# Backward pass of two attention blocks on one core: dwo rows in a shared ring of four, an earlier load of the second block's x^T and g^T, and small moves at both ends

## The chip, the cores and the metric

The kernel runs on one core of a Trainium2 chip. A core has a matrix engine (TensorE, PE in the profile; its weight loads are PEld), VectorE (DVE), ScalarE (ACT), GpSimd (POOL), and SyncE (SP), which here does nothing but issue transfers. Sixteen DMA engines move the data between HBM and the on-chip memory SBUF; matmuls write to PSUM, which has eight banks. The metric is the device time of one execution in microseconds, as the median of several runs.

## The reference

Two independent attention blocks, A and B, have the same shapes: batch 8, 96 queries, width 640, 32 heads of 128, 512 cached keys per head. All inputs are bf16.

```python
q = (x @ wq).reshape(B, Sq, H, Dh).transpose(0, 2, 1, 3)
scores = einsum("bhqd,bhkd->bhqk", q, k_cache) * Dh ** -0.5
p = softmax(scores)
o = einsum("bhqk,bhkd->bhqd", p, v_cache)
out = o.transpose(0, 2, 1, 3).reshape(B, Sq, H * Dh) @ wo
```

The outputs of both blocks are joined on the last axis. The kernel must return this output and, for a given gradient g of it, the gradients of all ten inputs: dx, dK, dV, dwq and dwo of A and of B. dK and dV are as large as the caches (33.5 MB each), so most traffic is the caches in and their gradients out.

## The kernel before

**Cells.** The unit of work is a cell: one head of one batch element, 256 per block and 512 in all. In a cell TensorE computes the scores S (L313), P^T and O^T (L360, L367), dV (L385), dP and the row sums dl (L409, L411), dQ^T and dS^T (L428, L435) and dK (L451). VectorE takes the row maximum, the reciprocal of the row sum, copies O^T and dS^T out of PSUM and forms dS. ACT does the exponential E and copies P^T, dV, dQ^T and dK out of PSUM. POOL scales E to P (L344) and forms the product of O^T and dO^T (L399).

**Ticks.** The order of the work is written by hand. Every piece is a function put on a list with a tick and a slot within the tick (`em.add`); the list is sorted and the functions run in that order. One cell starts per tick; its stages are spread over the following nine (`OFF`: scores at +3, P^T and dV at +4, O^T at +5, dP at +6, dK at +8, dQ^T at +9). Block 1 starts at tick 20 and block 2 at tick 276. The two heads of a pair alternate. The work of a whole head lies between the cells: transposes of wo and wq (`pB`, L214), Q^T and dO^T (`pC`, L231), their natural layouts (`pD`), and after the cells O and dQ in natural layout (`qA`), dwo (`qB`, L479), dwq (`qD`), and the sums over heads for the output and dx (`gU`, L526), in groups of four heads. Its ticks are offsets from the head's first tick, in the tables `HK`, `HK1`, `HK2` and `HKE`; `HKE` serves heads 30 and 31 of block 1. The framework then orders the instructions of each engine by priority, those of S, E and P before others, and makes an instruction that needs a new buffer wait until the last user of the old one has finished. Each engine carries out its instructions in order.

**Queues.** All transfers go through SP, in the order of the list: `Chain` (L62) ties each to the one before. A transfer that waits, or takes long to issue, holds all later ones. K^T and V^T are loaded by transposing transfers (L276), K and V as they are (L287), dV and dK are stored per pair of cells (L296). dV has four buffers, dK three.

**Buffers that matter here.** A ring of three buffers of [128, 640] bf16, named `ob`, holds the staged rows of g for block 2 (`setup_stage`, L137), the transposed wo of the first two heads, and the output rows of the last group of each block (`gU`, L537). The dwo rows have one buffer of that size, `dwo_sb` (L484): ACT fills it in two pieces (widths 128 and 512), SP stores it (L495) a tick or two later, and the next head's first piece must wait for that store to land. For most heads the first piece lies eight ticks after the last head's; for heads 29 and 30 of block 1 it is five (ticks 277 and 282), and head 29's row is stored at the start of tick 282.

**The handover.** Block 2 needs x^T (five transposing loads, `setup_xT`, ticks 262 to 266) and g^T. For g^T the six row tiles of g are loaded into `ob` at ticks 264 (three) and 269 (three) and transposed by TensorE four ticks later (`setup_T`, ticks 268 and 273). x^T and g^T have one buffer each, so they are loaded after the last use by block 1, in `pC` of head 31 (ticks 259 to 262).

**The start.** TensorE first transposes the row tiles of x against the identity (`tp_ps`, L158), then computes Q^T (`q_ps`, L249).

Of the kernel before, what the change touches and what calls it, by code (L numbers as in the profile page):

```python
# [7 lines left out]
ACT = mybir.ActivationFunctionType  # L8
ALU = mybir.AluOpType
# [35 lines left out]
HP = 2  # L45
# [4 lines left out]

HK1 = [dict(HK[0], pB=2, pC0=[-8, -6], pC1=[3, 3], pD1=3.5, pD0=6), dict(HK[1], pB=2, pC0=[-8, -6], pC1=[3, 3.6], pD1=4, pD0=7)]
HK2 = [dict(HK[0], pB=-5, pC0=[-6, -4], pC1=[-1, 0], pD1=1, pD0=2, qB=[28, 27]), dict(HK[1], pC0=[-2, 0], pC1=[1, 2])]
HKE = [dict(HK[0], qB=[23, 22]), dict(HK[1], qA0=25, qA1=27, qB=[29, 28], qD=[(30, 0, 2), (31, 2, 4), (32, 4, 5)])]
GT0, NG0, NX0 = 0, 15, 18
EV = dict(pB0="act", pB1="dve", pC00="act", pC01="act", pC10="act", pC11="dve", pD0="dve", pD1="dve", qA0="dve", qA1="dve", qB0="act", qB1="act", qD="dve", gU="act")
GSPREAD0 = 9
# [20 lines left out]
def build_block(tc, em, tick0, blk, x, kc, vc, wq, wo, g_all, out_all, dx, dk, dv, dwq, dwo, ident, ones, pools, HG=4, first=True, groups=None):  # L77
# [58 lines left out]

    def setup_stage(t):  # L137
        def f():
            S[("g_nat", t)] = wk.tile([128, D], BF16, name="ob", bufs=3)
            sp(nc.sync.dma_start(S[("g_nat", t)][:], g_flat[t * 128:(t + 1) * 128, :]))  # L140
        return f

# [33 lines left out]
    if first:  # L176
        for t in range(TT):
            late = t * 128 >= tsplits[0][1]
            em.add(tick0 - 15, SL_LOAD + (2 if late else 0), setup_nat(0, t, t + 1))
            em.add(tick0 - (7 if late else 9), SL_HEAD, setup_T(0, t))  # L180
            em.add(tick0 + GT0, SL_LOAD - 2, setup_nat(1, t, t + 1))
            em.add(tick0 + GT0, SL_HEAD + (2 if late else -1), setup_T(1, t))
    else:
        for c in range(DC):
            em.add(tick0 - 14 + c, SL_LOAD + 0.5, setup_xT(c))
        for t in range(TT):
            tt = tick0 - 8 + 5 * (t // 3)
            em.add(tt - 4, SL_LOAD + 0.5, setup_stage(t))
            em.add(tt, SL_HEAD - 1, setup_T(1, t))
        for t in range(TT):  # L190
            em.add(tick0 + NG0 + t, SL_LOAD + 0.5, setup_nat(1, t, t + 1))
            em.add(tick0 + NX0 + 2 * t, SL_LOAD + 0.6, setup_nat(0, t, t + 1))
# [21 lines left out]
    def pB(h):  # L214
        def f():
            st = HS[(blk, h)]
            woT_ps = bank([128, DC * 128], BF16, "woT_ps")
            for c in range(DC):
                nc.tensor.transpose(woT_ps[:, c * 128:(c + 1) * 128], st["wo_h"][:, c * 128:(c + 1) * 128], ident[:])
            woT_h = wk.tile([128, D], BF16, name="ob", bufs=3) if first and h < HP else hd.tile([128, D], BF16, name="woT_h", bufs=1)  # L220
# [118 lines left out]
    def c_s3b(h, b):  # L339
        def f():  # L340
            with tc.high_priority(PRIO_OFF):
                st = CS[(blk, h, b)]
                P_sb = wk.tile([Sq, Sk], BF16, name="P_sb", bufs=5)
                nc.gpsimd.tensor_scalar(P_sb[:], st["E_sb"][:], st["rinv"][:], 0.0, op0=ALU.mult, op1=ALU.add)  # L344
                st["P_sb"] = P_sb
        return f

# [70 lines left out]
    def c_s78(k8, k7):  # L418
        def f():
            x_ps = bank([128, 1024], BF16, "dq_dst_ps")  # L420
            dq_view = None
            if k8 is not None:
                st = CS[(k8[0], k8[1], k8[2])]
                hs = HS[(k8[0], k8[1])]
                tok = slice(k8[2] * Sq, (k8[2] + 1) * Sq)
                dQT_ps = x_ps[:, 0:2 * Sq].bitcast(F32)
                for c in range(KC):
                    nc.tensor.matmul(dQT_ps, st["K_sb"][:, c, :], st["dST_sb"][:, c * Sq:(c + 1) * Sq], start=(c == 0), stop=(c == KC - 1))  # L428
                dq_view = (dQT_ps, hs, tok)
            if k7 is not None:  # L430
                st7 = CS[(k7[0], k7[1], k7[2])]
                dS_sb = st7["dS_sb"]
                dST_ps = x_ps[:, 256:256 + KC * Sq]
                for c in range(KC):
                    nc.tensor.transpose(dST_ps[:, c * Sq:(c + 1) * Sq], dS_sb[:, c * 128:(c + 1) * 128], ident[0:Sq, 0:Sq])  # L435
                dST_sb = wk.tile([128, KC * Sq], BF16, name="dST_sb", bufs=3)
                nc.vector.tensor_copy(dST_sb[:], dST_ps)  # L437
                st7["dST_sb"] = dST_sb
            if dq_view is not None:
                dQT_ps, hs, tok = dq_view  # L440
                nc.scalar.activation(hs["dQT_h"][:, tok], dQT_ps, ACT.Identity, scale=scale)
        return f

    def c_s7(h, b):
# [34 lines left out]
    def qB(h, di):  # L479
        def f():  # L480
            st = HS[(blk, h)]
            Onat = st["Onat"]
            if "dwo_sb" not in st:
                st["dwo_sb"] = hd.tile([128, D], BF16, name="dwo_sb", bufs=1)  # L484
            dwo_sb = st["dwo_sb"]
            (c0, w) = dsplits[di]
            w_ps = bank([128, w], F32, "dwo_ps")
            for t in range(TT):
                nc.tensor.matmul(w_ps[:], Onat[:, t, :], S["g_nat"][:, t, c0:c0 + w], start=(t == 0), stop=(t == TT - 1))  # L489
            evac(EV["qB%d" % di], dwo_sb[:, c0:c0 + w], w_ps[:])  # L490
        return f
# [33 lines left out]
    def gU(g, which, t, di):  # L525
        def f():  # L526
            acc = S.get("out_acc" if which == 0 else "dx_acc")
            (c0, w) = dsplits[di]
            o_ps = bank([128, w], F32, "o_ps")
            for hh in range(groups[g]):  # L530
                h = GH0[g] + hh
                src = HS[(blk, h)]["OT_h"] if which == 0 else HS[(blk, h)]["dQT_h"]
                rhs = G[g]["wo_r"][:, hh, c0:c0 + w] if which == 0 else HS[(blk, h)]["wqT_h"][:, c0:c0 + w]
                nc.tensor.matmul(o_ps[:], src[:, t * 128:(t + 1) * 128], rhs, start=(hh == 0), stop=(hh == groups[g] - 1))  # L534
            if g == NG - 1:
                if di == 0:
                    G[(g, which, t)] = wk.tile([128, D], BF16, name="ob", bufs=3)  # L537
                dst = G[(g, which, t)][:, c0:c0 + w]
            else:
                dst = acc[:, t, c0:c0 + w]  # L540
            if g == 0:
                evac(EV["gU"], dst, o_ps[:])
            else:
                nc.vector.tensor_tensor(dst, o_ps[:], acc[:, t, c0:c0 + w], op=ALU.add)
        return f
# [80 lines left out]
def _kernel_impl(tc, A_x, A_k_cache, A_v_cache, A_wq, A_wo, B_x, B_k_cache, B_v_cache, B_wq, B_wo, grad_out,  # L626
# [13 lines left out]
    with ExitStack() as ctx:  # L640
        P = lambda **kw: ctx.enter_context(tc.tile_pool(**kw))
        cst = P(name="gconst", bufs=1)
        ident = cst.tile([128, 128], BF16, name="ident")
        make_identity(nc, ident[:])
        ones = cst.tile([128, 1], BF16, name="ones")
        nc.vector.memset(ones[:], 1.0)
        pools = dict(
            const=P(name="const", bufs=1),
            ps=P(name="ps", bufs=8, space=PSUM),
            kvp=P(name="kv", bufs=11),  # L650
            wk=P(name="wk", bufs=3),
            hd=P(name="hd", bufs=2),
            hst=P(name="hst", bufs=8),
            grp=P(name="grp", bufs=1),
        )
        pools["sp"] = Chain(tc)
        pools["S45"] = {}
        pools["S78"] = {}
        pools["HS"] = {}
        pools["CS"] = {}  # L660
        em = Emitter()
        t_next = 20
        for blk, args in enumerate(((A_x, A_k_cache, A_v_cache, A_wq, A_wo, grad_out, out_0, out_1, out_2, out_3, out_4, out_5),
                                    (B_x, B_k_cache, B_v_cache, B_wq, B_wo, grad_out, out_0, out_6, out_7, out_8, out_9, out_10))):
            H_ = args[1].shape[1]
            if blk == 0:
                grps = groupsA
# [72 lines left out]
```

## Time and profile before

| | |
|---|---|
| time, median of 5 runs | 1644.88 us (1640.71 to 1646.73) |
| the profiled execution | 1644.44 us, span 1642.7 us |
| mean granted TensorE clock | 0.996 |
| TensorE busy, idle in the span | 1611.6 us, 31.1 us |
| VectorE, ACT, POOL busy | 1337.4, 1350.8, 534.8 us |
| moved by DMA | 458.12 MB, mean 279 GB/s |
| store of a dwo row, issue to landing | 1.8 / 4.5 / 6.7 us (least, median, most) |
| transfers of the ring `ob`, issue to landing | 1.8 / 3.5 / 5.6 us |

The page gives one execution: busy time by engine, the chain of work that ended last, and groups of instructions with their mean duration and what ended the idle time before them. A row of the waits reads "engine, line waited for, releaser: total us, times, longest". A row of the timeline begins with the start and length in us; a bracket at its end is the idle time of that engine just before and what ended it. A row of the windows gives a stretch, its length, the busy time of PE, PEld, DVE, ACT and POOL with numbers of instructions, the granted TensorE clock (1 is full), the busy share of the DMA engines and GB/s.

### The profile page before, as it was taken

The numbers are of one execution on the slowest core, as the hardware profiler recorded it, in microseconds if no ns is written. First come the engines' busy times: TensorE is split into PE (matmuls) and PEld (weight loads), VectorE is DVE, ScalarE is ACT, GpSimd is POOL, SyncE is SP. The second block draws the span as 40 slices with busy tenths as digits, with TensorE's granted clock in tenths as the row PEclk, the third lists the DMA queues.
The fourth block names the chain that finished last, engine by engine and source line by source line (L and its number), as shares of the span: only waits on it lengthen the run. The fifth ranks groups of instructions, "written<-read, shape, count | busy, mean of one in ns | idle before, by whom it ended". The sixth has DMA issues, their size and how long they took to land.

```text
span 1642.7 us, 55592 instructions
## 1 busy us (share of the span) xinstructions
PE 1611.6 (98%) x20890; PEld 1261.4 (77%) x20890; DVE 1337.4 (81%) x3386; ACT 1350.8 (82%) x3514; POOL 534.8 (33%) x1030
## 2 busy tenths in 40 slices
PE   8999999999999999999989999999999999999998
PEld 5787877878777777777767777777787777877776
DVE  5786888888888888888768778888888888888896
ACT  6898988879788788888768889788798888889783
POOL 2332333333333333333223333333333333333331
PEclk9999999999999999999999999999999999999999
DMA  9999999999999999999999999999999999999994
GB/s 257 267 283 277 284 290 293 274 290 262 285 290 283 290 264 290 286 292 254 298 276 279 286 289 287 289 286 289 284 291 282 285 285 278 278 295 267 284 271 163
DMA packets 375566, 458.12 MB, mean 279 GB/s; under 512 B 40704, under 2 KB 367104, under 8 KB 367104
## 3 DMA queue, kind: packets, MB, share of 16 engines
q1 hardware_dynamic: 375296, 454.57, 102.5%
q8 instruction: 163, 2.67, 0.7%
q14 instruction: 107, 0.88, 0.1%
HBM read 160.10 MB, written 159.12 MB: 194 GB/s over the span
## 4 chain that ended last, share of the span: by engine, by line
PE 90%; ACT 4%; DMA 2%; DVE 1%; issue 1%; POOL 1%; SPq 0%; ACTq 0%; DVEq 0%
PE o_ps L534 12%; PE q_ps L249 12%; PE dV_ps L385 6%; PE dK_ps L451 6%; PE dwq_ps L509 6%; PE dwo_ps L489 6%; PE S_ps L313 6%; PE dP_ps L409 6%; PE optp_ps L360 6%; PE optp_ps L367 5%; PE dq_dst_ps L428 5%; PE dq_dst_ps L435 5%; PE n_ps L264 3%; PE nat_ps L475 3%; ACT E_sb L325 1%
## 5 line engine op out<-in xcount | busy, mean ns | idle before, releaser
L399 POOL TENSOR_TENSOR prod<-OT_h,dOT_h 128x96 bf16<-128x96 bf16 x512 | 187.1, 366 | 812.4 <-DVE rinv L335 452.8
L344 POOL TENSOR_SCALAR P_sb<-E_sb,rinv 96x512 bf16<-96x512 bf16 x512 | 352.4, 688 | 264.6 <-DVE rinv L335 264.2
L456 ACT ACTIVATE dK_sb<-dK_ps 128x512 bf16<-128x512 f32 x512 | 306.2, 598 | 141.9 <-PE dK_ps L451 126.4
L315 DVE TENSOR_REDUCE negm<-S_ps 96x1 f32<-96x512 f32 x512 | 347.7, 679 | 68.0 <-PE S_ps L313 67.6
L325 ACT ACTIVATE E_sb<-S_ps,negm 96x512 bf16<-96x512 f32 x512 | 352.1, 688 | 61.3 <-DVE negm L315 47.9
L413 DVE SCALAR_TENSOR_TENSOR dS_sb<-dP_ps,dl_ps,P_sb 96x512 bf16<-96x512 f32 x512 | 380.6, 743 | 1.1 <-PE optp_ps L367 0.8
L390 ACT ACTIVATE dV_sb<-dV_ps 128x512 bf16<-128x512 f32 x512 | 308.2, 602 | 4.6 <-PE dV_ps L385 2.6
L374 ACT ACTIVATE PT_sb<-optp_ps 128x384 bf16<-128x384 bf16 x512 | 256.2, 500 | 2.2 <-DVE OT_h L371 1.4
L437 DVE COPY dST_sb<-dq_dst_ps 128x384 bf16<-128x384 bf16 x512 | 177.8, 347 | 55.5 <-PE dq_dst_ps L435 53.9
L409 PE MATMUL dP_ps<-VT_p,dOT_h 128*96 128x512 bf16 x512 | 196.1, 383 | 4.9 <-ACT dwo_sb L169 4.9
L385 PE MATMUL dV_ps<-dOnat_h,P_sb 96*128 96x128 bf16 x2048 | 200.0, 219 | 0.0
L451 PE MATMUL dK_ps<-Qnat_h,dS_sb 96*128 96x128 bf16 x2048 | 199.0, 219 | 0.0
L313 PE MATMUL S_ps<-KT_p,QT_h 128*96 128x512 bf16 x512 | 194.2, 379 | 1.1 <-ACT dK_sb L456 0.4
L451 PEld LDWEIGHTS <-dS_sb 96*128 96x128 bf16 x2048 | 147.6, 97 | 48.4 <-issue 0.6
L367 PE MATMUL optp_ps<-ident,P_sb 96*128 96x96 bf16 x2048 | 172.6, 206 | 3.5 <-POOL P_sb L344 3.3
L428 PE MATMUL dq_dst_ps<-dST_sb,K_sb 128*128 128x96 bf16 x2048 | 172.0, 205 | 2.4 <-ACT dK_sb L456 2.4
L360 PE MATMUL optp_ps<-PT_sb,V_sb 128*128 128x96 bf16 x2048 | 169.6, 204 | 4.7 <-ACT PT_sb L374 2.6
L435 PE MATMUL dq_dst_ps<-ident,dS_sb 96*128 96x96 bf16 x2048 | 172.0, 205 | 0.0
L534 PE MATMUL o_ps<-wqT_h,dQT_h 128*128 128x512 bf16 (+1 forms) x768 | 149.3, 299 | 0.0
L534 PE MATMUL o_ps<-wo_r,OT_h 128*128 128x512 bf16 (+1 forms) x768 | 149.3, 299 | 0.0
L360 PEld LDWEIGHTS <-V_sb 128*128 128x128 bf16 x2048 | 107.7, 96 | 51.2 <-issue 3.9
L249 PE MATMUL q_ps<-xT,wq_p 128*128 128x256 bf16 (+1 forms) x640 | 135.4, 330 | 2.2 <-DMA wq_p<-in_A_wq_dram 1.4
(71 smaller groups left out, 3056.4 us busy)
## 6 DMA issues: line engine op xcount, KB each, us to landing
out_dram<-dV_sb SPq DMA_DIRECT2D x256, 256.0 KB, 4.4
out_dram<-dK_sb SPq DMA_DIRECT2D x256, 256.0 KB, 4.3
V_sb<-in_A_v_cache_dram SPq DMA_DIRECT2D x128, 256.0 KB, 4.4
K_sb<-in_A_k_cache_dram SPq DMA_DIRECT2D x128, 256.0 KB, 4.1
V_sb<-in_B_v_cache_dram SPq DMA_DIRECT2D x128, 256.0 KB, 4.1
K_sb<-in_B_k_cache_dram SPq DMA_DIRECT2D x128, 256.0 KB, 4.3
out_dram<-dwo_sb SPq DMA_DIRECT2D x64, 160.0 KB, 4.5
out_dram<-dwq_sb SPq DMA_DIRECT2D x32, 320.0 KB, 4.5
```

The source lines that it names most:

```text
L249: nc.tensor.matmul(q_ps[:], lhs(c), rhsT[:, c, t0:t0 + w], start=(c == 0), stop=(c == DC - 1))
L315: nc.vector.tensor_reduce(negm[:], S_ps[:], axis=AX.X, op=ALU.max, negate=True)
L325: nc.scalar.activation(E_sb[:].rearrange("q (a f) -> q a f", f=F4), st["S_ps"][:].rearrange("q (f a) -> q a f", f=F4), ACT.Exp, bias=st["n ...
L344: nc.gpsimd.tensor_scalar(P_sb[:], st["E_sb"][:], st["rinv"][:], 0.0, op0=ALU.mult, op1=ALU.add)
L360: nc.tensor.matmul(OT_ps, st["V_sb"][:, c, :], st["PT_sb"][:, c * Sq:(c + 1) * Sq], start=(c == 0), stop=(c == KC - 1))
L385: nc.tensor.matmul(dV_ps[:, c * 128:(c + 1) * 128], P_sb[:, c * 128:(c + 1) * 128], hs["dOnat_h"][:, b * 128:(b + 1) * 128], start=True, s ...
L390: nc.scalar.activation(dV_p[:, j], dV_ps[:], ACT.Identity, scale=1.0)
L409: nc.tensor.matmul(dP_ps[:], hs["dOT_h"][:, tok], st["VT"], start=True, stop=True)
L413: nc.vector.scalar_tensor_tensor(dS_sb[:].rearrange("q (a f) -> q a f", f=F4), dP_ps[:].rearrange("q (f a) -> q a f", f=F4), dl_ps[:, 0:1] ...
L451: nc.tensor.matmul(dK_ps[:, c * 128:(c + 1) * 128], dS_sb[:, c * 128:(c + 1) * 128], hs["Qnat_h"][:, b * 128:(b + 1) * 128], start=True, s ...
L456: nc.scalar.activation(dK_p[:, j], dK_ps[:], ACT.Identity, scale=1.0)
L534: nc.tensor.matmul(o_ps[:], src[:, t * 128:(t + 1) * 128], rhs, start=(hh == 0), stop=(hh == groups[g] - 1))
```

## The change

The ring `ob` has four buffers instead of three, and the dwo rows of all heads are taken from it; their own buffer is gone, so the memory is the same. Block 2's x^T is loaded at ticks 259, 260, 262, 263 and 265, its g rows at 261 and 266, and g is transposed at 265 and 270. To free x^T and g^T in time, heads 30 and 31 of block 1 do their transposes, Q^T and dO^T one to four ticks earlier, and head 31's wo is loaded three ticks earlier. At the start TensorE multiplies the identity by itself sixteen times into a PSUM bank that nobody reads. P of the first four cells (two heads, two batch elements) is scaled on VectorE instead of POOL. In the 16 cells of heads 30 and 31 of block 2, dQ^T is scaled and copied out of PSUM by VectorE instead of ACT.

```diff
-HKE = [dict(HK[0], qB=[23, 22]), dict(HK[1], qA0=25, qA1=27, qB=[29, 28], qD=[(30, 0, 2), (31, 2, 4), (32, 4, 5)])]
+HKE = [dict(HK[0], pB=-8, pC0=[-7, -6], pC1=[-6, -5], qB=[23, 22]),
+       dict(HK[1], pA=-10, pB=-4, pC0=[-4, -3], pC1=[-3, -2], pD1=2, pD0=5, qA0=25, qA1=27, qB=[29, 28], qD=[(30, 0, 2), (31, 2, 4), (32, 4, 5)])]
...
-            S[("g_nat", t)] = wk.tile([128, D], BF16, name="ob", bufs=3)
+            S[("g_nat", t)] = wk.tile([128, D], BF16, name="ob", bufs=4)
...
         for c in range(DC):
-            em.add(tick0 - 14 + c, SL_LOAD + 0.5, setup_xT(c))
+            em.add(tick0 - 17 + (3 * c) // 2, SL_LOAD + 0.5, setup_xT(c))
         for t in range(TT):
-            tt = tick0 - 8 + 5 * (t // 3)
+            tt = tick0 - 11 + 5 * (t // 3)
             em.add(tt - 4, SL_LOAD + 0.5, setup_stage(t))
             em.add(tt, SL_HEAD - 1, setup_T(1, t))
...
-                nc.gpsimd.tensor_scalar(P_sb[:], st["E_sb"][:], st["rinv"][:], 0.0, op0=ALU.mult, op1=ALU.add)
+                eng = nc.vector if first and h < HP and b * HP + h < 4 else nc.gpsimd
+                eng.tensor_scalar(P_sb[:], st["E_sb"][:], st["rinv"][:], 0.0, op0=ALU.mult, op1=ALU.add)
...
-                nc.scalar.activation(hs["dQT_h"][:, tok], dQT_ps, ACT.Identity, scale=scale)
+                evac("dve" if k8[0:2] in pools["light"] else "act", hs["dQT_h"][:, tok], dQT_ps, scale)
...
-                st["dwo_sb"] = hd.tile([128, D], BF16, name="dwo_sb", bufs=1)
+                st["dwo_sb"] = wk.tile([128, D], BF16, name="ob", bufs=4)
...
-                    G[(g, which, t)] = wk.tile([128, D], BF16, name="ob", bufs=3)
+                    G[(g, which, t)] = wk.tile([128, D], BF16, name="ob", bufs=4)
...
+        warm_ps = pools["ps"].tile([128, 128], F32, name="warm_ps", tag="bank")
+        for _ in range(16):
+            nc.tensor.matmul(warm_ps[:], ident[:], ident[:], start=True, stop=True)
         pools["sp"] = Chain(tc)
+        NH = A_k_cache.shape[1]
+        pools["light"] = {(1, h) for h in range(NH - HP, NH)}
```

More of the change, by code (lines that the diff above doesn't have):

```diff
@@ L219, in f @@
                 nc.tensor.transpose(woT_ps[:, c * 128:(c + 1) * 128], st["wo_h"][:, c * 128:(c + 1) * 128], ident[:])
-            woT_h = wk.tile([128, D], BF16, name="ob", bufs=3) if first and h < HP else hd.tile([128, D], BF16, name="woT_h", bufs=1)
+            woT_h = wk.tile([128, D], BF16, name="ob", bufs=4) if first and h < HP else hd.tile([128, D], BF16, name="woT_h", bufs=1)
             evac(EV["pB0"], woT_h[:], woT_ps[:])
```

## The prediction

> **What bounds the kernel now.** I read the page's sums first, then TensorE's waits, then the timeline where those waits lie, then SP's rows there, then the tail by windows.
>
> ```profile
> PE 1611.6 (98%) x20890; PEld 1261.4 (77%) x20890; DVE 1337.4 (81%) x3386; ACT 1350.8 (82%) x3514; POOL 534.8 (33%) x1030
> PE 90%; ACT 4%; DMA 2%; DVE 1%; issue 1%; POOL 1%; SPq 0%; ACTq 0%; DVEq 0%
> ...
> PE dP_ps L409 <- ACT dwo_sb L169: 4.9, 1, 4.9
> PE dq_dst_ps L428 <- ACT dK_sb L456: 2.4, 1, 2.4
> PE woT_ps L219 <- ACT dK_sb L456: 2.2, 1, 2.2
> PE tp_ps L158 <- DMA ob<-in_grad_out_dram: 1.2, 1, 1.2
> ```
>
> The first two lines are engine sums and the chain of waits: TensorE is the bound, so an edit gains only what it takes out of TensorE's idle time or out of slow-clock time. The other lines are single waits (total, times, longest). The edits aim at a few microseconds in three places.
>
> ```profile
> 782.15 2.19 SPq L140 DMA_DIRECT2D ob<-in_grad_out_dram  x3
> 786.78 1.28 PE L158 MATMUL tp_ps<-ident,ob 128*128 128x128 bf16 x15 [1.22 <-DMA ob<-in_grad_out_dram]
> 791.49 0.60 ACT L456 ACTIVATE dK_sb<-dK_ps 128x512 bf16<-128x512 f32 x1 [3.11 <-DMA out_dram<-dK_sb]
> 792.13 0.60 PE L219 MATMUL woT_ps<-ident,wo_r 128*128 128x128 bf16 x5 [2.15 <-ACT dK_sb L456]
> ...
> 821.12 1.15 SPq L495 DMA_DIRECT2D out_dram<-dwo_sb  x1
> 826.24 0.28 ACT L169 ACTIVATE dwo_sb<-dwo_ps 128x128 bf16<-128x128 f32 x1 [7.50 <-DMA out_dram<-dwo_sb]
> 826.57 0.58 PE L409 MATMUL dP_ps<-VT_p,dOT_h 128*96 128x512 bf16 x1 [4.88 <-ACT dwo_sb L169]
> ```
>
> This is the timeline where block 1 hands over to block 2 (start, length, engine; in brackets the idle time and its releaser). At 821.12 SP issues the store of one dwo row. ACT's next dwo evacuation needs the only dwo buffer, so it sits 7.50 us until that store lands, and TensorE runs dry for 4.88 us.
>
> ```profile
> 788.80:792.20 3.40, 1.25 (x25) 1.03 (x23) 1.27 (x4) 0.71 (x2) 0.36 (x1) 1.00 1.03 210
> 792.20:795.70 3.50, 3.50 (x17) 1.90 (x17) 1.90 (x4) 2.30 (x7) 0.69 (x1) 0.51 1.06 286
> 823.00:826.40 3.40, 0.00 (x0) 0.00 (x0) 0.00 (x0) 0.16 (x1) 0.00 (x0) 1.00 0.92 300
> 826.40:829.80 3.40, 3.23 (x19) 1.91 (x19) 0.99 (x3) 2.38 (x7) 1.05 (x2) 0.50 1.08 352
> ```
>
> In these windows (PE, PEld, DVE, ACT, POOL busy, granted clock, DMA share, GB/s) each of the two long gaps is followed by 3.4 us at clock 0.50. Work of 3.4 us at half clock needs 1.7 us at full clock: each costs 1.7 us more than its gap.
>
> **How late SP is.** All transfers go through SP in emission order. I measure its lag against the S_ps matmul of the tick before the one a transfer was emitted in. The first x^T load of block 2 (tick 262) was issued 6.7 us after that mark, the last g^T rows (tick 269; mark 768.3) 13.8 us after, at 782.15. SP's rows there follow each other within 0.1 us. So SP gains nothing while TensorE is on time; 11 extra loads are what put it behind, and TensorE's stalls give the time back.
>
> **Part 1, dwo rows in the ring.** Removed: the one-buffer wait. With four slots, dwo of head 30 (tick 282) no longer needs the landing of head 29's row. Gain 4.88 + 1.7 = 6.6 us. What is late next: the ring is now shared. The six outputs of the last group (ticks 282 to 289) reuse a slot about two ticks after their store; in the old ring of three the first was evacuated by 822.2, stored at 827.5 and reused at 837.6, which is 10.1 us after its issue against a median landing of 3.5 us for these rows: some 6.6 us of spare. SP's lag was -3.1 us at tick 285 because of the stall; without it, it starts 6.6 us higher. SP's rows of ticks 285 to 295 hold some 8 us of waiting beyond the usual 0.1 us between rows, so the lag drains by about tick 295, before the x and g loads of ticks 291 to 304 bring it back to 14. I take the whole 6.6. Bounds: 0 (all given back) and 6.6.
>
> **Part 2, x^T and g^T three ticks earlier, heads 30 and 31 with them.** Every instruction stays; 11 transfers move past the K, V, dK and dV transfers of ticks 259 to 268. SP's work up to tick 274 is the same sum, and so is TensorE's (columns summed from the code: at most 3.2 us ahead, at tick 257, and level again by tick 274). The g rows keep their lead of 4 ticks. Replaying SP's row lengths in the new order, the last g rows are issued at 773 to 775 and land near 778 by the 2.9 us that the last one took, while TensorE reaches their transposes near 776. That is a stall of about 2 us in place of 0.5 (V_sb at 778.8), 0.2 and 1.2; the store of dK at tick 270 comes at 786.2 in both orders, so ACT's 3.1 us and TensorE's 2.15 us stay. I take 0. Bounds: -5.8 if all of it goes (0.5 + 0.2 + 1.2 + 2.15 + 1.7), +3.7 for one more 2.0 us stall with its slow window. Queued behind a late slot on ACT are E, P^T, dV and dK of the next cell, for which TensorE waits; head 28's dwo (tick 269) needs the slot of head 27's, whose store the replay puts 1.3 us later.
>
> [...] Here a gap of 2.15 us was followed by a slow window. [...]
>
> **Part 3, sixteen dummy matmuls.** ident is ready near 1.3 us and the first x tile lands at 2.92. At the 107 ns between the early 128-column matmuls they last 1.7 us, to about 3.1. The first five transposes are 0.2 us later, hidden by the wait for the next tile (4.08).
>
> ```profile
> 7.31 3.94 PE L249 MATMUL q_ps<-xT,wq_p 128*128 128x512 bf16 x10 [1.45 <-DMA wq_p<-in_A_wq_dram]
> ```
>
> Seven of these ten start 427 ns apart, against 217 ns for the last: slow clock until 10.6 us. If the dummies woke the clock, they would save 7 x 0.21 = 1.5 us. The 1.8 us of transposes just before did not wake it; a window 87% busy after the gap at 70 us did not either (0.50 in 75.5 to 78.9), while 95% busy (826.4 to 829.8) did. Dummies and transposes fill at most 90% of any 3.4 us. I take 0; bounds -1.5 and +0.3.
>
> [...]
>
> **Part 4, P of four cells on VectorE.** No SBUF-to-SBUF VectorE row of this size exists; between 0.15 us (reciprocal, 96x1) and 0.69 (the 96x512 reduce), and nearest to the 0.49 of a 128x640 copy, against 0.69 on POOL and about 0.25 us of start. TensorE's wait of 1.6 us for P at 23.73 shrinks by 0.3 us at 0.49. It buys nothing in the end: at 72.50 TensorE waits 2.43 us for ACT, which waits for a dK store that SP issued at 66.29, some 13 us late. SP sets that moment, and has been issuing back to back since the start, so TensorE arriving earlier waits longer. 0; bounds -1.6 (that cover gone) and +1.4 (4 x 0.35 in front of VectorE's reduces).
>
> [...]
>
> **Part 5, dQ^T of 16 cells from ACT to VectorE.**
>
> ```profile
> 1595.00:1600.00 5.00, 4.95 (x76) 3.99 (x74) 4.10 (x12) 5.00 (x15) 1.80 (x5) 1.00 1.06 272
> 1600.00:1605.00 5.00, 4.16 (x65) 3.50 (x65) 4.76 (x13) 4.77 (x14) 2.73 (x6) 1.00 1.08 345
> 1605.00:1610.00 5.00, 4.28 (x74) 3.70 (x71) 4.38 (x12) 4.90 (x15) 2.06 (x4) 1.00 0.76 260
> ```
>
> From 1590 to 1611 ACT is full and TensorE idles some 2.3 us. By the distance between starts a cell costs ACT 2.12 us (E 0.66, PT 0.37, dV 0.48, dK 0.48, dQ^T 0.13) and VectorE 1.86 (0.63, 0.08, 0.18, 0.67, 0.30). Moving dQ^T gives 1.99 and, at the 0.18 of the like OT copy, 2.04. Some ten cells x 0.08 = 0.8 us; I take 0.7. Bounds -2.3 (all the idle time) and +2 (VectorE, 89% busy from 1590 to 1610, late for ten cells by 0.2).
>
> **The sum** against the profiled execution: 1644.44 - 6.6 - 0.7 = 1637.1 us (its span is 1642.7; 1.7 lie around it). That execution is 0.44 below the median shown, 1644.88. The five runs span 1640.7 to 1646.7, so 0.2% (3.3 us) is about what can be told from no change: faster means below 1641.6.
>
> **The rivals.** (a) *A new wait takes the old one's place*: the 2 us stall near 776 lasts long enough for a slow window, 3.7 us; for it, the g rows' unchanged lead and the shared slot; against it, TensorE stood at most 2 us there. 1640.8; with part 1's late stores on top to 1645. (b) *The handover clears as well*: SP catches up in the heavier ticks 252 to 257 and dK's store is on time: 1637.1 - 5.8 = 1631.3; against it, SP was never idle there. (c) *Slower*: the ring holds up the last group. Its twelve output tiles are evacuated by VectorE, in order before reduces and dS. Without the 4.88 us stall the stores leave up to 6.6 us later and the spare is 6.6: if SP's lag doesn't drain from tick 285 and the landing is dwo's longest, 6.7 us, instead of 3.5, each tile waits 1 to 1.5 us: +12 to +18 - 7.3 gives 1649 to 1655. It decides once the lag at ticks 285 to 296 stays above 6 us. For it, dwo rows now hold slots in these ticks too; against it, SP's 8 us of waiting. (d) *The change doesn't do what it says*: dwo of head 30 gets a slot whose store is as late; 1644.4 - 0.7 = 1643.7.
>
> **How the numbers follow.** Forecast 0.53 (own range 1634 to 1640.5), (a) 0.19, (b) 0.08, (c) 0.15, (d) 0.05. Faster: forecast, (b) and 0.04 of (a): 0.65. Same: the rest of (a) and (d), 0.20. Slower: 0.15. Range: 1632 leaves out half of (b), 1648 leaves out (c): 1632 to 1648.
>
> **What would show it.** Right: no ACT wait for out_dram<-dwo_sb near 820, no 0.50 clock there, VectorE's ob rows without DMA waits. Part 2 right: a stall near 776 and still one by dK near 790. Part 3 right: q_ps still 3.9 us for ten. The prediction is wrong if the slow window stays or a wait for ob appears on VectorE or ACT.

## The result, and the profile after

| | before | after |
|---|---|---|
| median, first comparison (88 and 47 runs) | 1646.51 us | 1642.53 us (1636.83 to 1651.38) |
| ratio, 95% interval | | 0.9978 [0.997, 0.9985] |
| the profiled execution | 1644.44 us | 1641.74 us |
| its span | 1642.7 us | 1640.0 us |

The change saves 0.22%, some 3.6 us; the forecast was 7.3 us. A second comparison of the same pair (below) gave 0.9967 [0.995, 0.9983]. The time lies in the range given; the gain is about half of what was forecast.

To see where it went I compare the two profiled executions by the start of each tick's S matmul. A step is what TensorE gains (-) or loses (+) against before within a stretch, the first one counted from the start of the span:

| ticks | to 250 | 250 to 283 | 283 to 285 | 285 to 293 | 293 to 320 | 320 to 534 | to the end | sum |
|---|---|---|---|---|---|---|---|---|
| step, us | +1.18 | +0.43 | **-6.59** | **+1.03** | **+2.44** | -0.65 | -0.53 | -2.69 |

The ring delivers its 6.6 us at the place foreseen, and 3.5 us of them are returned in the next 35 ticks. First the page of after, engine sums and chain, then rows of its waits (total, times, longest):

```profile
PE 1612.9 (98%) x20906; PEld 1262.2 (77%) x20906; DVE 1340.2 (82%) x3406; ACT 1348.3 (82%) x3498; POOL 532.3 (32%) x1026
PE 90%; ACT 4%; DMA 3%; DVE 1%; issue 1%; SPq 0%; POOL 0%; ACTq 0%; DVEq 0%
```

```profile
PE dwo_ps L491 <- ACT dK_sb L458: 3.4, 3, 2.0
ACT ob L170 <- DMA out_dram<-ob: 3.0, 1, 3.0
DVE ob L546 <- DMA out_dram<-ob: 2.9, 1, 2.9
...
PE tp_ps L159 <- DMA ob<-in_grad_out_dram: 2.2, 1, 2.2
...
PE woT_ps L220 <- ACT dK_sb L458: 1.3, 1, 1.3
...
PE dV_ps L387 <- DVE ob L546: 0.9, 1, 0.9
```

TensorE is the bound as before. The wait of 4.88 us for dwo is gone; two waits for the ring have come, one on ACT and one on VectorE. TensorE's waits for ACT's copy of dK add up to 9.8 us, against 6.2 before; the largest increase is in dwo_ps (3.4, before 0.3), while the wait of woT_ps shrank from 2.2 to 1.3. The timeline shows where (idle time and its releaser in brackets):

```profile
779.90 0.28 ACT L170 ACTIVATE ob<-dwo_ps 128x128 bf16<-128x128 f32 x1 [2.96 <-DMA out_dram<-ob]
...
780.25 0.91 PE L159 MATMUL tp_ps<-ident,ob 128*128 128x128 bf16 x10 [2.22 <-DMA ob<-in_grad_out_dram]
...
795.00 0.44 PE L220 MATMUL woT_ps<-ident,wo_r 128*128 128x128 bf16 x5 [1.28 <-ACT dK_sb L458]
...
820.25 0.27 ACT L170 ACTIVATE ob<-dwo_ps 128x128 bf16<-128x128 f32 x1
...
823.13 0.38 PE L411 MATMUL dP_ps<-VT_p,dOT_h 128*96 128x512 bf16 x1
...
844.61 0.69 DVE L546 TENSOR_TENSOR ob<-o_ps,out_acc 128x512 bf16<-128x512 f32 x1 [2.91 <-DMA out_dram<-ob]
...
845.36 0.38 PE L387 MATMUL dV_ps<-dOnat_h,P_sb 96*128 96x128 bf16 x4 [0.86 <-DVE ob L546]
...
919.03 0.60 ACT L458 ACTIVATE dK_sb<-dK_ps 128x512 bf16<-128x512 f32 x1 [2.24 <-DMA out_dram<-dK_sb]
919.68 0.38 PE L491 MATMUL dwo_ps<-g_nat,Onat 128*128 128x512 bf16 x1 [2.01 <-ACT dK_sb L458]
```

Rows 820.25 and 823.13 have no bracket: dwo of head 30 and the dP behind it start at once. At 844.61 VectorE waits for the store of an older output tile, and the reduce behind it comes late; at 919.03 ACT waits for a store of dK.

**The DMA engines are the reason.** The four windows are ticks 283 to 285, 285 to 295, 295 to 305 and 305 to 320 (stretch, length, busy time of PE, PEld, DVE, ACT, POOL, granted clock, DMA share, GB/s). Before:

```profile
820.57:833.38 12.81, 7.93 (x76) 5.43 (x75) 5.04 (x13) 4.23 (x11) 1.09 (x3) 0.87 1.06 313
833.38:870.43 37.05, 37.05 (x457) 28.39 (x455) 29.56 (x75) 28.51 (x73) 11.04 (x21) 1.00 0.95 261
870.43:897.42 26.99, 26.65 (x368) 20.88 (x366) 25.11 (x66) 24.46 (x65) 9.79 (x20) 1.00 1.05 290
897.42:945.72 48.30, 46.31 (x599) 36.10 (x598) 36.50 (x90) 40.81 (x110) 15.99 (x32) 1.00 1.05 285
```

After:

```profile
822.17:828.41 6.24, 6.24 (x77) 4.59 (x76) 4.96 (x13) 4.04 (x10) 1.10 (x3) 1.00 0.75 231
828.41:866.49 38.08, 37.22 (x457) 28.43 (x455) 29.56 (x75) 28.39 (x73) 11.03 (x21) 1.00 1.09 299
866.49:894.73 28.24, 26.96 (x368) 20.86 (x367) 25.04 (x66) 24.35 (x65) 10.16 (x21) 1.00 1.02 302
894.73:944.21 49.48, 46.29 (x598) 36.06 (x598) 36.68 (x91) 41.23 (x111) 15.65 (x31) 1.00 1.06 286
```

Rate times length, added up: before moves 35.3 MB in 125.15 us (282 GB/s), after 35.5 MB in 122.04 us (291 GB/s). Before, the DMA engines kept working through TensorE's stall (share 1.06), and then had too little to do for 37 us (0.95, 261 GB/s). After, the share is 0.75 for the 6.24 us in which TensorE no longer stalls and above 1 from then on; over the first two windows together it is 1.04, against 0.98 before. The ring moved TensorE's work forward by 6.6 us; the transfers had little more than this dip of 37 us to move forward into. How little the engines had to spare shows in the rest of the two traces: laid end to end from 0 to 1560 us, the thirteen stretches of 120 us move 267 to 288 GB/s in before (283 in the median, shares of 1.01 to 1.06) and 265 to 293 in after (284, 1.02 to 1.07). The 291 GB/s of after in these ticks is close to the top.

### The profile page after: what moved, and what is told of

The parts are those of the page before. It is cut to its first block, busy times and chain, and to the rows that moved or that the text cites. A ratio compares the mean times of both kernels' runs of the same rounds, so it can differ in the third digit from the quotient of the medians.

```text
span 1640.0 us, 55580 instructions
## 1 busy us (share of the span) xinstructions
PE 1612.9 (98%) x20906; PEld 1262.2 (77%) x20906; DVE 1340.2 (82%) x3406; ACT 1348.3 (82%) x3498; POOL 532.3 (32%) x1026
## 4 chain that ended last, share of the span: by engine, by line
PE 90%; ACT 4%; DMA 3%; DVE 1%; issue 1%; SPq 0%; POOL 0%; ACTq 0%; DVEq 0%
PE o_ps L536 12%; PE q_ps L250 12%; PE dwq_ps L511 6%; PE dK_ps L453 6%; PE dV_ps L387 6%; PE dwo_ps L491 6%; PE S_ps L314 6%; PE dP_ps L411 6%; PE optp_ps L362 5%; PE optp_ps L369 5%; PE dq_dst_ps L430 5%; PE dq_dst_ps L437 5%; PE n_ps L265 3%; PE nat_ps L477 3%; DMA out_dram<-dK_sb 2%; ACT E_sb L326 1%
## 5 line engine op out<-in xcount | busy, mean ns | idle before, releaser
L491 PE MATMUL dwo_ps<-g_nat,Onat 128*128 128x128 bf16 (+1 forms) x768 | 135.9, 300 | 3.4 <-ACT dK_sb L458 3.4
```

## The experiments

All kernels were profiled once and timed in five rounds. The table has the steps against the profiled execution of before, as above, and the ratio to before with its interval. Kernels of one comparison share a chip; between comparisons before itself had medians of 1653.76 (A), 1658.45 (B), 1646.63 (C) and 1647.06 us (D).

| kernel | to 250 | 250-283 | 283-285 | 285-293 | 293-320 | ratio |
|---|---|---|---|---|---|---|
| A ring alone | +6.58 | +6.37 | -6.59 | +2.48 | +2.92 | 0.9983 [0.9963, 1.0003] |
| A two own dwo buffers | +7.05 | +2.57 | -6.59 | 0.00 | +0.87 | 0.9986 [0.9965, 1.0008] |
| A lead alone | +6.47 | +0.69 | +1.79 | 0.00 | -0.23 | 0.9991 [0.9975, 1.0008] |
| A changed, old start | +10.14 | +5.10 | -6.59 | 0.00 | +5.61 | 0.9984 [0.9967, 1.0001] |
| B before, no x and g rows | +7.35 | -0.44 | +2.15 | 0.00 | -0.30 | 0.9966 [0.9949, 0.9982] |
| B changed, no x and g rows | +5.82 | +2.60 | -6.59 | +1.88 | -2.53 | 0.9935 [0.991, 0.996] |
| B changed, two own dwo buffers | +6.38 | +4.60 | -6.59 | +3.93 | +6.91 | 0.9942 [0.992, 0.9965] |
| B changed, four dK buffers | +5.39 | +1.67 | -6.59 | +2.81 | +3.57 | 0.9957 [0.9936, 0.9979] |
| C changed, again | -2.64 | -1.69 | -6.59 | +1.44 | +3.19 | 0.9967 [0.995, 0.9983] |
| C changed, x and g rows merged | +0.71 | +0.58 | -6.59 | +2.25 | +2.86 | 0.9962 [0.9944, 0.998] |
| C changed, balanced leads | -0.96 | -1.80 | -6.59 | +4.06 | +2.06 | 0.9936 [0.9913, 0.9959] |
| D changed, earlier stores | +2.04 | +1.39 | -6.59 | 0.00 | +3.74 | 0.9966 [0.995, 0.9982] |
| D balanced, earlier stores | -2.60 | -3.16 | -6.59 | 0.00 | +2.74 | 0.9928 [0.9911, 0.9945] |

The first two columns vary by 10 to 13 us between executions. The two kernels whose code up to tick 250 is that of before (lead alone, before without the rows) reach tick 250 6.5 and 7.4 us later than its one execution. Much of this goes with the comparison: the first column is +5.4 to +10.1 in A and B, where before itself is 7 and 12 us slower than in the first comparison, and -2.6 to +2.0 in C and D. So one execution says nothing on the start and little on the handover. The third column is the same to 0.01 us in all eleven rows with a second slot for dwo.

### The parts alone

The ring alone:

```diff
-... name="ob", bufs=3) ...
+... name="ob", bufs=4) ...
...
-                st["dwo_sb"] = hd.tile([128, D], BF16, name="dwo_sb", bufs=1)
+                st["dwo_sb"] = wk.tile([128, D], BF16, name="ob", bufs=4)
```

> The kernel before with part 1 alone: the ring ob of four, dwo rows taken from it. Theory 'given back': between ticks 283 and 285 TensorE is 6.6 us earlier than before (no idle 4.88 us and no half-clock window near 826), SP's lag is higher by as much, and some 3.4 us come back by tick 313: about 1.0 at tick 291 through VectorE's ob tiles waiting for the store of an older ob tile, the rest through ACT's dK waiting for stores of dK. End: 3 us below before, ratio 0.998. Rival 'the other parts cost it': nothing comes back after tick 285, the end is 6 to 6.6 us below before, ratio 0.996, and the start and the handover of the whole change cost the other 3 us.

Measured: -6.59 at tick 283, and +5.4 us by tick 320, 2.5 of them on VectorE's ob tiles. The rival, that the ring keeps its gain and other parts cost the 3 us, falls: nothing but the ring is in this kernel.

The lead alone (the lines of `setup_xT`, `setup_stage`, `setup_T` and `HKE` of the change, nothing else):

> The kernel before with part 2 alone: x^T and g^T of block 2 three ticks earlier and heads 30 and 31 with them; dwo keeps its single buffer, the ring has three. Theory 'moved, not removed': a stall of about 2.2 us near 778 (transposes waiting for the last g rows) in place of 0.5, 0.2 and 1.2, the dK stall after it smaller, by tick 277 0 to 0.6 us later than before, and the 4.88 us at tick 283 stays, shifted by that. End within 1 us of before, ratio 0.9995 to 1.0005. Rival 'the lead costs part of the ring's gain': 2 to 4 us above before. Rival 'the lead clears the handover': 3 to 6 us below before, no tp_ps wait over 0.5 us.

Measured: two waits of TensorE for g rows (0.47 and 1.58 us), the same dK wait (2.15 us at 797), +0.69 over the handover, the dwo stall left (5.32 us). Nothing comes back after tick 285, as in before. The lead moves the stalls and clears none; so "moved, not removed" holds, as far as one execution and an interval of 0.3% can tell.

The changed kernel with the start of before (no dummies, P of four cells on `nc.gpsimd`):

> The changed kernel without its start: no dummy matmuls, P of the first four cells on GpSimd as before. Theory 'absorbed': TensorE loses 0.4 us by tick 39 against the changed kernel and has it back after the wait near 70 us, because SP sets that moment; from tick 80 on within 0.3 us of the changed kernel, end within 1 us of it (1642.5). Rival 'the start costs': in the changed kernel the waits near 70 and 107 us are longer (2.88 and 0.91 us) because TensorE comes earlier to stores that are no earlier; without the start parts they shrink to 2.4 and 0.2 and the end is about 1.2 us below the changed kernel. Rival 'the start pays': the end is 0.5 to 1.5 us above the changed kernel.

Measured: between ticks 23 and 39 it gains 0.03 us on before, the changed kernel 0.39; so P on VectorE is worth some 0.4 us there. What comes after is open: the waits near 70 and 107 us are 2.44 and 1.07 us here, but over all executions the first is 2.4 to 3.1 us with P on GpSimd and 2.6 to 3.4 us with P on VectorE in the kernels with three dK buffers and the old leads. The rivals differ by 1 us, less than this scatter, and less than the interval.

### What gives the time back

Block 2's x and g rows in natural layout (twelve loads, 1.97 MB) are the extra transfers of ticks 291 to 304. Two kernels leave them out and use block 1's rows, so their dwq and dwo of block 2 are not the reference's and only their times count:

```diff
-        for t in range(TT):
-            em.add(tick0 + NG0 + t, SL_LOAD + 0.5, setup_nat(1, t, t + 1))
-            em.add(tick0 + NX0 + 2 * t, SL_LOAD + 0.6, setup_nat(0, t, t + 1))
```

> The kernel before without the twelve loads of block 2's x and g rows in natural layout (ticks 291 to 304; 1.97 MB); dwq and dwo of block 2 are computed from block 1's x and g instead, so these two outputs are not the reference's. Theory 'the transfers set the pace': before, SP waited 11 us in ticks 285 to 294 and lost nothing by it, because its lag was -3 us; with less to move the lag at tick 303 falls from 9 us to about 3 us, TensorE's small idle gaps of ticks 300 to 310 (some 1.9 us) shrink, and the end is 1 to 2 us below before, ratio 0.999. Rival 'these loads don't matter': the end is that of before within 0.3 us.

> The changed kernel without the same twelve loads (dwq and dwo of block 2 come from block 1's x and g, so these two outputs are not the reference's). Theory 'the transfers set the pace': the ring's 6.6 us at tick 283 are given back in ticks 289 to 313 only because SP and the DMA engines are busy without a break there; with 1.97 MB less the lag at tick 303 is 5 to 7 us instead of 12.3, the idle gaps of ticks 302 to 313 (2.4 us) don't come back, and against the kernel before without the same loads TensorE keeps 4.5 to 6 us at tick 320 where the full kernels keep 3.1 us. End 0.995 to 0.997 of before. Rival 'shared slots': the wait of VectorE for an old ob tile at tick 291 (1.0 us) and the late dK stores come back all the same, and the pair without the loads differs by the same 3.1 us as the full pair.

Windows of the changed kernel without the loads, the same four stretches:

```profile
828.99:835.22 6.23, 6.18 (x76) 4.58 (x76) 4.96 (x13) 4.04 (x10) 1.10 (x3) 1.00 0.86 281
835.22:874.14 38.92, 36.91 (x451) 28.44 (x455) 29.56 (x75) 28.41 (x73) 11.08 (x21) 1.00 1.04 284
874.14:901.14 27.00, 26.50 (x366) 20.83 (x367) 25.10 (x66) 24.49 (x65) 9.82 (x20) 1.00 1.05 288
901.14:946.90 45.76, 45.11 (x594) 35.85 (x599) 36.13 (x90) 40.70 (x110) 16.02 (x32) 1.00 1.05 280
```

33.4 MB in 117.91 us, still at 283 GB/s and a share over 1: with 2 MB less to move the stretch is 4.1 us shorter than in the changed kernel. SP's lag, measured as in the prediction:

| tick | 286 | 288 | 294 | 296 | 303 | 313 |
|---|---|---|---|---|---|---|
| before | -0.8 | -0.6 | -2.2 | 2.8 | 9.0 | 10.4 |
| changed | 8.0 | 8.5 | 1.4 | 5.1 | 12.3 | 10.8 |
| changed, no x and g rows | 8.5 | 9.3 | 0.4 | 2.4 | 7.3 | 9.4 |
| changed, rows merged | 8.6 | 9.2 | 0.9 | 5.3 | 13.6 | 11.0 |

Of the ring's 6.59 us this kernel keeps 7.2 at tick 320 (-6.59 + 1.88 - 2.53: small idle gaps that before has there went too). What the changed kernel loses in ticks 293 to 320 (2.4 us) is not lost here; the loss near tick 290 behind VectorE's wait, ahead of these loads, stays (1.88 us). This is one execution, and the fastest of the six of its kernel (1644.31 us, median 1648.79). The times say less: by their ratios to before, each kernel without the loads is 0.3 to 0.4% below its full counterpart, more than the first expectation had, and the pair differs by 4.4 us, within what full pairs differ by. The trace of before without the loads doesn't show where it gains; that is open.

The same bytes in two transfers instead of twelve:

```diff
+        em.add(tick0 + NG0 + 2, SL_LOAD + 0.5, setup_nat(1, 0, TT))
+        em.add(tick0 + NX0 + 5, SL_LOAD + 0.6, setup_nat(0, 0, TT))
```

> The changed kernel with block 2's x rows and g rows in natural layout loaded by one transfer each (g at tick 293, x at tick 299) instead of six each: the same 1.97 MB, ten transfers fewer to issue. Theory 'the bytes set the pace': the DMA engines are busy without a break in ticks 285 to 313 and the rows of SP only grow with their backlog, so the time comes back as in the changed kernel, 3 to 6 us between ticks 285 and 320, against -0.6 us without the loads; end within 2 us of the changed kernel on the same chip. Rival 'SP's issuing sets the pace': ten rows of about 0.55 us fewer take some 5 us off the lag at tick 303, under 1.5 us come back, and the end is 3 to 5 us below the changed kernel.

> The changed kernel once more, on the chip of the next two kernels: another execution to see what comes back after tick 285, and another ratio. Theory 'the transfers set the pace': 6.59 us gained between ticks 283 and 285 as in every execution with a second slot for dwo; between ticks 285 and 320 3 to 11 us come back (3.5, 5.4, 5.6 and 10.8 us so far), the more the later SP is at tick 286; ratio 0.995 to 0.999. Rival 'the loss of ticks 285 to 320 was chance': under 2 us come back in this execution.

Measured: ten rows fewer on SP, and the lag at tick 303 is 13.6 us, not 7; 5.1 us come back, against 4.6 in the changed kernel beside it. SP's own rows show why the number of transfers didn't matter here: in ticks 285 to 294 the changed kernel's 46 rows take 32.8 us (34.2 in the execution beside it), the 42 of the merged kernel 34.9 us. The merged load itself is issued in 0.46 us, like a small one; the other 41 rows take 34.4 us instead of 30.6 (32.0). What is saved on the number of rows comes back in the length of the others, as it would if the queue waits for the DMA engines.

### The shared ring, or late stores

Two dwo buffers of their own, output tiles and g rows in a ring of three, on the kernel before and on the changed one:

```diff
-                st["dwo_sb"] = hd.tile([128, D], BF16, name="dwo_sb", bufs=1)
+                st["dwo_sb"] = hd.tile([128, D], BF16, name="dwo_sb", bufs=2)
...
-... name=key + "_p", bufs=5 if which == 0 else 4)
+... name=key + "_p", bufs=4)
```

> The kernel before with two dwo buffers of their own, the ring ob left at three for the g rows and the output tiles; the memory for it is taken from K^T (four buffers instead of five). Theory 'given back through the shared ring': the 4.88 us and its half-clock window go as in the ring alone, the 1.0 us at tick 291 does not come back, because output tiles and dwo rows no longer queue for the same slots; the part that comes back through late dK stores (about 2.4 us at ticks 302 to 313) stays. End about 1 us below the ring alone (4 us below before). Rival 'SP's lag alone': the output tiles wait for their own late stores as well with three slots, the 1.0 us stays or grows, and the end is that of the ring alone or above. If four K^T buffers are too few, S waits for KT all along and the end is far above.

> The changed kernel with two dwo buffers of its own and a ring of three for g rows and output tiles (memory from K^T: four buffers instead of five). Theory 'shared slots cost 1 to 2 us': no wait of VectorE for an old ob tile at ticks 287 to 293, 0 to 1 us given back in ticks 285 to 313, as with two own buffers on the kernel before (0.9 us), against 3.5 us in the changed kernel; end 1 to 3 us below the changed kernel. Rival 'the transfers set the pace': the 1.0 us at tick 291 goes, but as much more comes back by tick 313, since SP's work is the same; 3 to 5 us given back in all, end within 1 us of the changed kernel.

The two runs contradict each other: 0.9 us back in the first, 10.8 in the second, 3.9 of it with this row (timeline of the second):

```profile
855.22 0.69 DVE L546 TENSOR_TENSOR ob<-o_ps,out_acc 128x512 bf16<-128x512 f32 x1 [4.13 <-DMA out_dram<-ob]
```

No dwo row can be in the way there. VectorE waits for a slot that one of its own output tiles still holds. The landings say which: in all eight executions with this wait, with a ring of three or of four, the fifth output tile starts 0.1 us after the store of the second (tick 286) has landed, in after at 844.61 behind 844.52. The second execution is also the slowest of the nine of its kernel (1658.74 us, median 1650.60), so its 10.8 us are an extreme. What differs between the two executions is how late SP is (lag at tick 288: 5.0 and 9.8 us) and how fast the DMA engines were over ticks 283 to 320 (294 and 284 GB/s). So the sharing is not the cause of this wait; my first reading, after the run on before, fell with the second run.

Earlier stores test the same thing from the other side:

```diff
-em.add(tk + 2, SL_LOAD + 0.3, gU_st(g, which, t))
+em.add(tk + 1, SL_LOAD + 0.3, gU_st(g, which, t))
```

> The changed kernel with the stores of the last group's output tiles put one tick earlier in the list (one tick after the tile's tick instead of two), for both blocks. Theory 'two prices': the wait of VectorE for an older ob tile near tick 291 (2.9 us idle on VectorE, 1.0 to 2.2 us on TensorE so far) goes or falls under 0.5 us, because each store leaves 3.1 us earlier; what comes back at ticks 301 to 320 through late transfers stays or grows by as much, since the bytes are the same; 2.5 to 5 us come back between ticks 285 and 320, end within 1.5 us of the changed kernel on other chips (ratio to before 0.996 to 0.998). Rival 'the slot wait is a loss by itself': 1 to 2 us less comes back, and the end is as much lower.

Measured: nothing is lost in ticks 285 to 293, and 3.74 us come back after that; before the edit it was 1.0 and 2.4, or 1.4 and 3.2 us, in sum 3.5 and 4.6. The ratio is that of the changed kernel (0.9966 and 0.9967). The wait on VectorE is one place where TensorE meets the late transfers; taken away alone, most of it is met at the next, as far as one execution can tell.

### A version that beats both

Each cell transfer has a lead: the ticks between its place in the list and the need for its data or its slot. In the changed kernel K^T has six, V^T and V four, K and dV five, dK's store four (three buffers). Four dK buffers alone:

```diff
-... name="dK_sb", bufs=3)
+... name="dK_sb", bufs=4)
...
-... name=key + "_p", bufs=5 if which == 0 else 4)
+... name=key + "_p", bufs=4)
```

> The changed kernel with four dK buffers instead of three (memory from K^T: four instead of five). Theory 'dK slots are where late stores bite': the waits of ACT's dK for stores of dK go (2.9 us and its half-clock windows near 70 us, 0.9 near 107, 1.3 at the handover, 2.0 near 918) and TensorE may lead SP by one pair more (lag up to 15 to 17 us instead of 11 to 13); end 4 to 8 us below the changed kernel, ratio to before 0.993 to 0.995. Rival 'the transfers set the pace': the same time is lost at the next thing that SP brings (V, K or K^T loads, O^T after V_sb), and the end is within 1.5 us of the changed kernel.

Measured: ACT no longer waits for a store of dK at any place, and waits for V come (O^T on V_sb 2.08 us at 119 and 1.69 at 71, dP on VT 2.57 at 923). At 0.9957 in a comparison that did not hold the changed kernel, its gain can't be told apart. The rival's mechanism is what the trace shows. Then the leads are made equal, five ticks each:

```diff
-OFF = dict(kt=-3, vt=2, vn=1, kn=4, dv=7, dk=10, ...
+OFF = dict(kt=-2, vt=1, vn=0, kn=4, dv=7, dk=11, ...
```

> The changed kernel with four dK buffers (memory from K^T, four instead of five) and the cell transfers moved so that each has five ticks from its place in the list to its need: K^T one tick later (2 before the cell's start instead of 3), V^T and V one tick earlier, dK's store one tick later. In the changed kernel these had six, four, four and four. Theory 'late transfers stall TensorE only where the lag of SP passes the shortest lead': TensorE may lead by one tick (3.1 us) more, the waits for V_sb, VT and for stores of dK near 70, 107, 795, 900 and 918 us shrink or go, also the half-clock windows behind those over 2 us; end 4 to 9 us below the changed kernel on the same chip. Rival 'the transfers set the pace all along': TensorE waits as long for the same bytes elsewhere, end within 1.5 us of the changed kernel.

Measured: 1637.26 us against 1640.85 for the changed kernel on the same chip, 3.6 us less, with intervals that overlap a little (0.9913 to 0.9959 and 0.995 to 0.9983). The two profiled executions would have said the reverse: against before the balanced one ends 4.5 us earlier, the changed one 7.6. ACT's waits for stores of dK are down to 2.2 us in all, but the ring's stretch gives back 6.1 us, 4.1 of them through two of VectorE's ob tiles. With the earlier stores on top:

> The changed kernel with four dK buffers, five ticks of lead for every cell transfer, and these stores one tick earlier. Without the earlier stores it gave back 4.1 us by tick 291 and 6.1 us by tick 320 and ended at a ratio of 0.994 to before. Theory 'two prices': the 4.1 us at ticks 287 to 291 fall under 1.5 us, 1 to 3 us of it come back later as waits of S for K^T; ratio 0.992 to 0.994. Rival 'the slot wait is a loss by itself': all 4.1 us are kept and the ratio is 0.991 or below.

Measured: 1634.43 us, against 1640.49 for the changed kernel with earlier stores and 1647.06 for before; 2.7 us come back instead of 6.1, all after tick 293. Its interval (0.9911 to 0.9945) lies below those of the changed kernel (0.995 upward in C) and of the one with earlier stores alone (D), so this version beats both kernels; its lead over the balanced kernel lies inside the intervals. Two of its rows of waits follow. In after, ACT waited 11.3 us for stores of dK and TensorE 9.8 us for ACT's copies of dK; here it is 2.2 and 0.5 us, and TensorE waits for K^T instead:

```profile
PE S_ps L314 <- DMA KT_p<-in_A_k_cache_dram: 3.1, 2, 2.0
...
ACT dK_sb L458 <- DMA out_dram<-dK_sb: 2.2, 2, 1.6
```

SP's lag reaches 15.8 us at tick 303 in this kernel, and TensorE loses 4.1 us at ticks 301 to 305; the changed kernel began to lose at 11 to 12 us.

## Why the prediction was wrong, and where it was right

**Part 1, the stall: right.** -6.59 us, in place and size, in all twelve executions with a second slot.

**Part 1, what is late next: wrong, and it decides.** The step that failed is "SP's rows of ticks 285 to 295 hold some 8 us of waiting beyond the usual 0.1 us between rows, so the lag drains by about tick 295 ... I take the whole 6.6". That waiting was made by the stall itself: SP had caught up (lag -3.1 us) and waited for TensorE. Without the stall SP waits 4.3 us in ticks 285 to 294 instead of 11.0, its rows there take 32.8 us instead of 30.4, and at tick 303 the lag is 12.3 us instead of 9.0. Of this waiting, 7.0 us were beyond the usual 0.1 us a row in before, and 8.6 and 10.5 us in the two other executions with the stall; in all twelve without it, 0.4 us are. The lag did fall, to 1.4 us at tick 294, but not to the -2.2 of before. I counted an idle time of SP as room, without asking what the DMA engines could carry: the window of before that showed a share of 0.95 for 37 us, among shares of 1.05 and 1.06, was the room: 0.10 of 37 us, by this estimate 3.7 us. The term should have been some 3 us: 6.6 less the 3.5 that came back. In the other executions with all the loads it was 0.9 and 10.8 us at the extremes, and 2.7 to 6.4 us in the other eight.

**Rival (c), "the ring holds up the last group": its mechanism came, at a fraction of its price.** The lag stayed at 5.4 to 8.5 us in ticks 285 to 290 and VectorE waited 2.91 us for a slot, TensorE lost 1.03 us. Priced was 12 to 18 us, with each of twelve tiles waiting. One tile waited: by tick 291 the lag was down to 4.3 us. And it is not the dwo rows in the ring, as the kernel with own dwo buffers and the landings show, but the late store of an output tile. The forecast's own sign, "a wait for ob appears on VectorE or ACT", appeared on both.

**Part 2: 0 forecast, +0.43.** The stall came as replayed, 2.22 us at 778.0 (about 2 near 776 was said), and the new wait of ACT for head 27's slot too (2.96 us). The wait for dK shrank to 1.28 us and its half-clock window went, where I had kept both; the half-clock window came behind the 2.22 us instead (782.0 to 785.4), which the forecast gave to rival (a). Two errors that cancel, so the right sum is luck. It is luck, too, that the measured 1641.74 us lies near the 1640.8 of rival (a): its stall and its half-clock window came, but in place of the window behind the dK wait, not on top of it. Other executions had -3.2 to +5.1 over the handover with the same lead and -0.4 to +6.4 without it, so what the lead is worth can't be told.

**Parts 3 and 4: 0 forecast, +1.18 by tick 250**, of which nothing can be put down to the edits, as the scatter of that column shows. P on VectorE takes 348 ns (688 on POOL), between my bounds and below the 0.49 us taken. The dummies did not wake the clock in the profiled execution, as I said (`q_ps` 3.94 us for ten). In other executions it was otherwise: see below. One reading there was off: the window after the gap at 70 us that I called 87% busy was 82% (2.88 of 3.50 us).

**Part 5: -0.7 forecast, -0.53 measured** between tick 534 and the end; -0.51 to -0.70 in every kernel that has it, -0.18 to +0.18 in those that have not.

**The sum** of the forecast was -6.6 - 0.7 = -7.3; the profiled execution shows -6.59 - 0.53 + 3.47 for what came back, + 1.61 before tick 283, - 0.65 after tick 320 = -2.69. The 3.47 is the error; the 1.61 is within what executions differ by, and the 0.65, nearly all of it by tick 345, was not followed up.

## What to carry to other kernels

Here one queue feeds everything and the DMA share stood at 1.02 over ticks 283 to 320 of before, and TensorE's stall of 4.88 us was also the time in which the queue caught up, to a lag of -3.1 us at tick 285. In a kernel that looks like this, before counting a stall as gain, add up the bytes of the stretch and divide by the rate that its neighbours reach. By 35.3 MB and the 285 to 290 GB/s of its last two windows, the stretch above could shrink from 125 us to some 122 to 124, an estimate; after took 122.0, and the executions with all the loads and a second slot 119.4 to 129.4. The room was nearer to the dip in the DMA share (3.7 us by the estimate above; the stretch became 3.1 us shorter) than to the idle time of the engine (4.88) or of the queue (11.0). What helped here was an equal lead for every transfer, with a fourth dK buffer and earlier stores, more than another slot for the one that stalled; what each of the three is worth, the runs can't tell apart.

## What the runs showed of the hardware

**The clock changed on a grid in these traces.** In before the granted clock changes at 18, 20, 229, 230, 239, 240 and 478 times 3.4133 us after its first full stretch begins (10.61 us), in after at 18, 20, 226, 227 and 477 times 3.4133 us (from 10.58 us). What TensorE did in the windows of this grid, between 15 and 1600 us of the two executions (busy time in us, in brackets the start of the window):

| clock in the window | TensorE busy, of 3.41 us: before | after | clock in the next |
|---|---|---|---|
| 1.00 | 0.00 (822.99), 1.27 (788.85), 1.29 (68.64) | 1.29 (68.61), 1.49 (778.57) | 0.50 |
| 1.00 | 1.82 (20.85), 2.11 (819.57), 2.19 (785.44) | 2.14 (792.23), 2.21 (20.82), 2.26 (918.53) | 1.00 |
| 1.00 | 2.74 or more (the other 454) | 2.51 or more (the other 456) | 1.00 |
| 0.50 | 2.85 (72.05) | 2.56 (72.02) | 0.50 |
| 0.50 | 3.24 (826.40), 3.41 (75.47), 3.41 (792.27) | 3.41 (781.99), 3.42 (75.43) | 1.00 |

So in these two executions what a gap cost went with where it fell. After, the 2.22 us gap at 778 lies mostly in one window and is followed by half clock; the 2.01 us gap at 917.7 straddles two (0.86 and 1.15 us) and is not. Windows of after:

```profile
778.57:781.98 3.41, 1.49 (x17) 1.18 (x18) 0.62 (x3) 2.08 (x7) 0.73 (x2) 1.00 0.91 169
781.99:785.40 3.41, 3.41 (x20) 1.91 (x18) 1.42 (x4) 2.79 (x6) 1.01 (x2) 0.50 1.27 392
```

1.49 of 3.41 us busy is 0.44, and the next window stands at 0.50. The prediction's flat 1.7 us per gap of 2 us was too simple: this window, with 1.92 us idle, was followed by half clock, the one of before at 20.85, with 1.60 us idle, was not.

**Whether the dummies at the start helped differed between executions.** With the same sixteen matmuls full clock began at 10.6 us in after, at 4.3 us in the changed kernel with earlier stores and at 4.2 us in the balanced one with earlier stores; in before, without them, at 10.6 us. In the balanced one TensorE was busy for all of the 2.84 us from 1.36 to 4.20; in after it was busy for 2.39, 1.98 and 3.28 us in the three windows of 3.41 us from 0.34, and full clock came behind the third. After, and then balanced with earlier stores:

```profile
7.30 3.94 PE L250 MATMUL q_ps<-xT,wq_p 128*128 128x512 bf16 x10 [1.42 <-DMA wq_p<-in_A_wq_dram]
...
6.58 2.33 PE L250 MATMUL q_ps<-xT,wq_p 128*128 128x512 bf16 x10 [0.73 <-DMA wq_p<-in_A_wq_dram]
```

It is 2.33 us for the ten matmuls that take 3.94 us after. In the execution with 4.3 us the clock fell to 0.50 at 7.7, after a window with 1.58 of 3.41 us busy. The balanced execution and two others with dummies were 1.8 to 2.4 us ahead of before at tick 23; by tick 100 two of the three had lost it again. Both are of comparison B, where a kernel with the start of before (without the rows) stood 3.8 us behind before at tick 100, and they 1.0 and 2.6 us; so the loss need not be that of the start.
